# The last 64 tokens of every batch as a ninth batch, and PSUM banks that start from a copy, in an attention and mixer kernel

## The chip, the cores and the metric

The kernel runs on one core of a Trainium2 chip. The metric is the device time of one execution in microseconds. Three runs gave 572.27, 292.12 and 291.67 us; the median is 292.12 us. The profiled execution took 292.22 us, of which the span from the first to the last instruction is 290.5 us. TensorE's granted clock was 1.000 over it.

## What is computed

Eight batches of 576 tokens with eight heads of width 64 go through a block-causal attention (blocks of 64 tokens) and then a mixer: a token MLP over the 576 tokens and a channel MLP over the 512 channels.

```
scores = q @ k.T / 8, masked to block_i >= block_j; attn = softmax(scores); x = attn @ v   # x: 8 x 576 x 512
h  = relu(x.T @ w_tok1) @ w_tok2          # tokens 576 -> 256 -> 576
u  = x + h.T
out = u + relu(u @ w_ch1) @ w_ch2         # channels 512 -> 1536 -> 512
```

Inputs and the output are float32 in HBM; matmul operands are bf16, sums are float32 in PSUM.

## The kernel before

All work is recorded as operations with a list of engines, a cost, what they depend on, a priority, and the PSUM banks that they take and give back. A planner (`Plan.run`) then plays the engines forward on those costs and writes out one fixed order for each engine; the chip runs each engine's list in that order, and semaphores hold an instruction until what it needs is there. `SHIFTS` moves each operation's priority, and `ONLY` ties an operation that may go to VectorE or ScalarE to one of them. So an edit of the operations re-orders everything.

**Attention.** A batch is done in two groups of four heads. q and k come by GpSimd's DMA queue (L491) into `raws`, three buffers each, and VectorE transposes them 32 by 32 into `turned` (L514), three buffers each. TensorE makes scores in 32-row tiles (L638), ScalarE takes exponentials (L656), VectorE copies and clears a corner of the tile (L664, L669, the "tail"), TensorE multiplies by v (L684, and L737 for the last 64 tokens), and VectorE divides (L704, L710, L759, L765).

**Token MLP.** L879 and L883 go up, L976 goes down, L991 adds x. A batch has 4 chunks of 128 tokens, and 64 tokens more. The 64 tokens of two batches make one chunk of 128 (L1007, L1016), called mixed. From the third batch on, u is transposed to `uT` (and `umT` for the mixed chunk) by DMA; before that by TensorE (L1065).

**Channel MLP, up.** Batches 0 to 3 use plain products, 48 matmuls of 512 columns each (L1102, evacuated with a relu by L865 or L867 into `gT`). Batches 4 and 5, and 6 and 7, go as pairs by Strassen's scheme with seven products in place of eight (`channel_up_fast`, L1207): twelve blocks in all, each of seven products of two 512-column matmuls into three banks a, c, e. Three times in a block a running sum is copied out of PSUM into float32 scratch (`keep`, L472 or L474), three times a bank is added to such a copy (`join`, L1235, VectorE alone), two clips apply the relu in SBUF (L1248, L1250), and one evacuation has the relu in it. The mixed chunks go up by 48 matmuls of 128 columns each (L1129).

**Channel MLP, down.** Batch 0 and the mixed chunks use plain products (L1422). Batches 1 to 7 use Strassen's scheme again (`channel_down_fast`, L1331): seven products of twelve 256-column matmuls, four operand sums on VectorE (L1315) into a ring of five `sums` buffers, and seven folds on VectorE (L1354) that add a bank into an output buffer of the ring `o_sb` (four buffers). Batch 7 does this in two halves of 128 tokens. SyncE issues the output DMAs (L1376, L1464, L1472).

**Banks.** PSUM has eight banks. Four are the ring `mm`; four hold score pairs (`sc`) until the last scores are done and are then the pool `late`. The weight sums that the up scheme needs (L1161) lie in the memory of `raws`, so they wait for the last transposes. At the start, filler matmuls on zeros (L444, L451) run while nothing else is ready.

Of the kernel before, what the change touches and what calls it, by code (L numbers as in the profile page):

```python
# [30 lines left out]
class Plan:  # L31
# [5 lines left out]
    FIRST = {"POOL": 2.2, "ACT": 0.7, "SP": 0.7}  # L37
    def __init__(self):
        self.ops = []
        self.free = {}  # L40
# [4 lines left out]
    def add(  # L45
        self, engines, cost, emit, deps=(), prio=0.0, take=(), give=(), xfer=None, mode=0, at=0.0,
        urgent=0, until=1e9, quick=False, stick=False,
    ):

        o = Op()  # L50
        o.engines = (engines,) if isinstance(engines, str) else tuple(engines)
        o.cost = cost if isinstance(cost, dict) else {e: cost for e in o.engines}
        o.emit, o.prio, o.take, o.give, o.xfer = emit, prio, take, give, xfer
        o.mode, o.at, o.urgent, o.until, o.quick, o.stick = mode, at, urgent, until, quick, stick
        o.deps = list({id(d): d for d in deps if d is not None}.values())
        o.users, o.n = [], len(self.ops)
        self.ops.append(o)
        return o

# [20 lines left out]
    def run(self):  # L80
        for o in self.ops:
            o.users = []
            need = {}
            for pools, _ in o.take:
                need[pools] = need.get(pools, 0) + 1
            o.need = list(need.items())
# [15 lines left out]
        while left:  # L102
# [13 lines left out]
            for e in ("PE", "ACT", "DVE", "POOL", "SP"):  # L116
# [33 lines left out]
                o.end = busy[e] = t + o.cost[e]  # L150
# [17 lines left out]
                for note in o.give:  # L168
                    heapq.heappush(gives, (o.end + lag * (not o.quick), note["pool"], note["slot"]))
# [14 lines left out]
    0 0 0 1086 0 0 -1796 0 0 -2204 0 0 -436 0 0 -2236 0 -874 1122 0 -1461 -716 0 -57 -676 0 -823 -356 -634  # L184
    -427 -327 -263 -1862 -1168 -1449 -2035 -910 -961 0 0 0 0 0 -455 -1706 1784 0 0 0 0 0 0 0 0 0 0 0 0 0 0 0 0
    0 0 0 0 0 0 0 0 0 0 0 0 0 0 0 0 0 0 0 0 0 0 0 0 0 0 0 0 0 0 0 0 0 0 0 0 0 0 0 0 0 0 0 0 0 0 0 0 0 0 0 0 0
    0 0 0 0 0 0 0 0 0 0 0 0 0 0 0 0 0 0 0 0 0 0 0 0 0 0 0 0 0 0 0 0 0 0 0 0 0 0 0 0 0 0 0 0 0 0 -1759 -2258
    -829 -1773 -745 -600 -518 -403 -408 -435 -478 -330 -234 -318 115 -707 -721 1449 901 360 -2687 1285 -1364
    -2663 -477 -1268 -1711 287 183 60 -1283 -954 -1917 -689 1260 -1321 -3156 -277 -2070 327 -4275 -2077 496
    -958 721 -1027 -4175 -2062 1142 -727 2194 -29 -1726 -2650 1829 285 -2440 -587 561 -1269 -2630 256 -371  # L190
    -2381 -1108 500 -834 1464 -234 -2459 -3607 -433 -116 -1181 -3036 -4652 757 -3135 -1190 1799 -2575 472 511
    -1937 2261 -2334 -1313 -80 283 -1168 -1950 43 -141 -572 904 -1435 -2531 -1785 -705 1388 1245 8 -529 -1166
    122 839 964 1422 961 460 980 153 587 -70 -1841 -1402 4368 1485 -233 -1066 -157 1316 3304 -4269 -2567 -609
    -37 -2795 -1857 -2628 2386 -953 -1988 756 121 794 -1179 508 -1540 396 993 414 1373 -628 3080 -1481 1693
    1380 2018 3179 1215 133 -1865 -30 -1438 310 -1741 1233 2110 3174 952 1308 1314 2083 -536 -1377 2942 3324
    3966 4046 -972 2806 2021 -985 1780 2009 2286 1063 -343 -501 3018 -221 -12 851 -3518 181 648 3044 777 -1559
    1331 2605 -1938 2510 -1273 1427 692 3242 642 3161 831 3827 1590 2498 1272 3666 1243 -521 1458 965 2312
    3170 1911 1539 456 1382 -395 1781 1291 412 1115 2033 407 -2584 203 1653 -37 -1067 651 390 632 712 2085
    1236 1774 1916 638 -351 1999 3579 1238 3795 2213 1760 2315 580 1733 1472 2148 32 1832 1928 3235 2037 1010
    1326 3512 2592 569 1322 795 233 4616 692 2264 1859 3321 2543 1003 -1446 -622 1012 5769 3912 3513 -1135  # L200
    3484 1816 1558 3086 1631 377 460 3746 131 2416 1317 3495 268 93 1492 -2200 1682 -1517 -1061 -1918 -804
    -2555 220 1892 -1350 -552 633 -602 -3011 2584 -1528 1015 -1345 -970 -279 205 -3142 -1238 490 -3231 1304
    -4554 -73 -1779 -1041 -2783 -2072 1282 -1760 -3094 -3999 -1158 -3686 -2285 -1138 2616 668 1259 1241 -1598
    167 2071 -909 858 -881 727 2164 -1678 1042 574 -585 -480 1799 -693 -2709 29 2701 348 589 1804 2316 358
    -243 1501 498 -1435 2925 2117 -1872 -1946 -1387 -550 71 3572 -327 523 -486 285 2909 1867 3747 1873 -3277
    -237 -2256 -2904 165 1714 -375 2033 1315 108 1985 908 -3282 871 -1113 -3213 -1928 456 -985 -2942 -1169
    -1109 -439 -1452 -1077 1083 4521 -657 -397 -1807 -1177 148 -136 72 -499 -383 2346 -1426 535 908 1654 -1908
    1556 -870 940 1384 760 3049 1518 1614 -388 -397 698 599 -1772 77 -1100 -188 -99 1679 -537 3661 -611 -4713
    -2779 -3471 -1192 4222 -2288 7 135 683 470 -124 -1937 4311 -1202 2026 3954 1883 -580 -144 -1263 -1252 213
    124 -1229 1816 -503 66 -1382 -2249 -465 -2153 -1738 2390 -2661 -24 -2228 -2001 -239 -409 -1529 -375 -1081  # L210
    -581 735 -984 38 -260 -2302 1217 -2261 -3269 -2251 -248 -4644 -204 -1377 -2426 -4000 -3533 -8 -1126 -1048
    1395 -1267 -1990 -1332 -2616 -192 -1101 44 -647 1960 -632 -3925 1998 -2860 -1766 -1304 1946 -86 -1897 1720
    -2063 220 166 1393 1695 678 281 1263 937 1502 1991 1492 1224 967 -2008 -3069 100 -1197 831 -2311 762 2963
    -2753 1116 -1491 772 -1270 -2454 -83 -684 517 2274 -199 924 -996 -335 -437 -4244 92 2836 34 1600 1818
    -1703 782 437 3822 -1486 158 903 133 149 -809 -2686 1861 1030 754 81 904 4463 -1403 3008 -481 2513 2124
    362 2078 2881 2322 87 45 1400 1014 -40 -952 494 -2798 1008 -114 697 3665 -1141 -790 980 3595 2615 768 1541
    2162 1088 350 4168 2791 198 819 1089 1662 127 -873 -1414 -1490 -607 1650 -475 -1425 155 -479 819 -205 3125
    1025 1982 -966 1282 523 1433 -866 2401 -1302 -2306 -1390 1706 -1061 492 -1463 362 -5 -382 4027 670 261
    -1148 3368 3865 226 2561 -27 918 1300 -1251 479 -1039 -942 377 1706 -1619 634 2612 294 -1198 -454 -443
    3079 257 2561 367 4603 1450 1230 175 3506 2620 1475 2517 1440 -455 1815 2349 469 1362 -2181 3618 1351 245  # L220
    2103 3448 -649 1023 -389 1673 1698 1565 3393 -672 -617 1513 1982 1900 -43 -2127 -515 177 1287 -662 3642
    435 -281 523 1100 -3212 -53 930 2250 -1503 -2709 -312 1997 -1218 -146 -1266 500 -430 -294 -3993 259 38
    3742 2116 492 3949 930 120 -982 1354 3674 845 2860 394 407 2113 2870 17 2438 -399 5223 4732 5550 4129 4822
    -33 2182 140 2669 2676 1714 -1974 3137 2139 597 3962 -795 -837 -175 1231 2212 -2167 872 1722 1254 1464
    2663 -1228 3092 1502 3237 3444 837 1937 1623 4494 3997 1526 2423 2361 3182 5805 -2367 3270 4613 6090 1790
    -279 1558 -1156 3445 2684 5301 1696 3189 2135 3585 4003 1969 -123 4948 2149 90 3310 -2135 1890 2816 3455
    3645 1607 1958 2568 1525 -862 -700 1980 4204 3729 2032 1434 102 -1352 1072 -305 329 2181 3132 -214 1770
    3447 1290 174 -1834 3312 -2908 2149 2971 -366 1171 1119 2325 -854 967 2462 -356 1390 9 1911 1872 1049 -29
    1500 -1830 879 -556 946 -2641 1129 89 -1773 630 -830 307 -726 612 -2751 -266 -369 -2652 -249 -2997 -2094
    -899 -3813 -1242 -82 -2802 -4725 -1627 -158 -2687 -3327 -1181 -2531 223 -1599 2803 -1175 -2176 -1434 -2276  # L230
    -4223 -5240 341 496 422 482 -3394 -3204 -2712 -2522 -2522 -1911 -658 -1781 -2177 653 0 -882 1808 55 1483
    -527 1255 -875 -780 -1430 -1339 427 -56 -728 -1932 -2188 1432 -2375 1447 -1541 -275 -412 1347 1940 -1648
    1054 -2047 -2930 -20 -638 -3394 -289 236 1329 -396 -1030 -2 -444 2933 1287 2625 1732 2239 -2641 1568 -100
    2268 1855 -176 2627 -458 1457 325 641 3791 -1272 2191 1450 850 1534 2275 1760 1242 3001 2749 4305 1003
    2517 -1573 -478 2960 949 -609 376 1575 1763 -2541 -909 -788 -97 -352 -310 862 -3721 -1923 635 -135 1667
    574 1186 2265 115 611 666 -636 1650 2081 -469 1899 -579 -251 -160 -1812 4751 1754 904 2662 2274 -443 4012
    415 477 1333 2156 1991 2662 2996 269 1798 748 3408 -2292 -1115 735 2456 2953 43 -2067 -63 -553 1093 719
    -283 929 -1465 841 -2035 -1822 -1363 -820 -2068 -704 -3580 -995 -5820 -1642 692 -1374 -1445 -1196 -624
# [29 lines left out]
def kernel(  # L268
# [11 lines left out]
    nc = tc.nc  # L280
# [1290 lines left out]
```

## Time and profile before

| | |
|---|---|
| Median of the runs shown | 292.12 us |
| Profiled execution, its span | 292.22 us, 290.5 us |
| TensorE busy | 283.6 us (98%), 3991 matmuls |
| VectorE busy | 242.3 us (83%) |
| ScalarE busy | 150.5 us (52%) |
| GpSimd busy | 62.4 us (21%) |
| Down products by Strassen (L1331) in the chain that ended last | 17.8% + 4.1% of the span |
| Plain up products (L1102) in it | 14.9% |
| Up products by Strassen (L1207) in it | 6.4% + 6.1% |
| Mixed chunk, up (L1129), in it | 3.5% |

Busy time is the time in which at least one of an engine's instructions ran. Matmuls overlap each other in the records, since each is listed from its start to the modelled end of its output, so the time that one costs is read from how far apart the starts of equal matmuls lie, not from its listed length. The chain that ended last is followed back from the last instruction to what released each step.

### The profile page before, as it was taken

Reading aid. Unit: us, or ns where it says so; the run is one execution under the profiler, and the core shown is the slowest. Engines: PE = TensorE matmul, PEld = TensorE weight load, DVE = VectorE, ACT = ScalarE, POOL = GpSimd, SP = SyncE. Lnnn points to the kernel's source line nnn. Section 1 sums busy time; section 2 is a strip of 40 time slices with the busy share of each in tenths; the row PEclk is TensorE's granted clock in tenths of the full one; section 3 lists DMA queues with packets and bytes.
Section 4 is the critical chain, followed back from the end, with each engine's and each line's share of the span. In section 5 each row is a group of like instructions: output and inputs, shape, how many; then the busy total and the mean of one; then the engine's idle time right before and its main releaser. Section 6 shows DMA issues by size and latency. Waiting matters only on the chain.

```text
span 290.5 us, 9147 instructions
## 1 busy us (share of the span) xinstructions
PE 283.6 (98%) x3991; PEld 186.4 (64%) x3991; DVE 242.3 (83%) x520; ACT 150.5 (52%) x196; POOL 62.4 (21%) x101
## 2 busy tenths in 40 slices
PE   8999999899999999999999999999999999999994
PEld 3576555556746676565877576875456897555884
DVE  3686498786899998789999866998999969999993
ACT  5985727487636556765576976503536102545000
POOL 9674455550170035142005000000000000000000
PEclk9999999999999999999999999999999999999999
DMA  7999999999299059989927800610101921310134
GB/s 234 210 167 202 211 194 192 224 189 161 45 103 178 0 89 192 190 121 172 81 76 99 60 2 2 93 74 9 64 20 24 150 45 74 144 72 2 37 112 180
DMA packets 64840, 32.67 MB, mean 112 GB/s; under 512 B 53152, under 2 KB 55328, under 8 KB 64800
## 3 DMA queue, kind: packets, MB, share of 16 engines
q0 software_dynamic: 44032, 16.75, 49.3%
q1 hardware_dynamic: 20768, 15.34, 21.7%
q8 instruction: 31, 0.51, 0.7%
q14 instruction: 9, 0.07, 0.1%
HBM read 35.85 MB, written 9.44 MB: 156 GB/s over the span
## 4 chain that ended last, share of the span: by engine, by line
PE 95%; DMA 2%; ACT 1%; DVE 1%; issue 1%; SPq 0%
PE mm L1331 18%; PE mm L1102 15%; PE sc L638 11%; PE mm L1422 7%; PE mm L684 7%; PE mm L1207 6%; PE late L1207 6%; PE mm L879 5%; PE late L1331 4%; PE mm L976 4%; PE mm L1129 3%; PE mm L737 3%; DMA gT<-in_q_dram 2%; PE mm L883 1%; PE mm L451 1%; PE mm L1007 1%
## 5 line engine op out<-in xcount | busy, mean ns | idle before, releaser
L656 ACT ACTIVATE e_sb<-sc 128x1024 bf16<-128x1024 f32 x95 | 92.2, 1023 | 44.4 <-PE sc L638 41.3
L1102 PE MATMUL mm<-uT,wc_sb 128*128 128x512 bf16 x192 | 46.6, 381 | 0.0
L540 POOL DMA_DIRECT2D vals<-in_v_dram x45 | 37.0, 834 | 39.3 <-PE mm L684 27.9
L514 DVE STREAM_TRANSPOSE turned<-raws 128x288 int32<-128x288 int32 (+1 forms) x65 | 40.6, 695 | 5.6 <-ACT raws L472 4.2
L638 PE MATMUL sc<-turned 32*64 32x64 bf16 (+7 forms) x1260 | 35.0, 292 | 0.5 <-DVE turned L514 0.5
L1102 PEld LDWEIGHTS <-wc_sb 128*128 128x128 bf16 x192 | 20.0, 115 | 16.5 <-issue 1.9
L638 PEld LDWEIGHTS <-turned 32*64 32x64 bf16 x1280 | 19.5, 104 | 14.5 <-issue 10.9
L684 PE MATMUL mm<-vals,e_sb 128*128 128x65 bf16 x630 | 25.9, 193 | 1.3 <-issue 1.3
L710 DVE TENSOR_TENSOR x_sb<-mm,rinv 128x256 bf16<-128x256 f32 x63 | 25.8, 420 | 1.3
L684 PEld LDWEIGHTS <-e_sb 128*128 128x128 bf16 x640 | 23.1, 97 | 5.6 <-issue 2.3
L1331 PEld LDWEIGHTS <-sums 128*128 128x128 bf16 x252 | 24.3, 98 | 3.4
L1331 PEld LDWEIGHTS <-gT 128*128 128x128 bf16 x240 | 22.8, 98 | 4.6 <-issue 0.4
L867 DVE TENSOR_SCALAR gT<-mm 128x512 bf16<-128x512 f32 x25 | 17.2, 689 | 9.5 <-PE mm L1102 9.1
L865 ACT ACTIVATE gT<-mm 128x512 bf16<-128x512 f32 x26 | 15.6, 600 | 6.0 <-PE mm L1102 4.8
L879 PE MATMUL mm<-x_sb,w_sb 128*128 128x512 bf16 (+1 forms) x88 | 17.1, 321 | 0.0
L1354 DVE TENSOR_TENSOR o_sb<-mm,u_sb 128x512 f32<-128x512 f32 x22 | 15.1, 686 | 2.1 <-PE mm L1331 1.9
L1331 PE MATMUL mm<-wd_sb,sums 128*128 128x256 bf16 x132 | 16.4, 273 | 0.0
L991 DVE TENSOR_TENSOR u_sb<-mm,x_sb 128x512 bf16<-128x512 f32 x23 | 15.2, 684 | 0.9 <-PE mm L976 0.7
L1207 PEld LDWEIGHTS <-raws 128*128 128x128 bf16 x96 | 9.2, 98 | 10.1 <-issue 0.2
L865 ACT ACTIVATE aT<-mm 128x512 bf16<-128x512 f32 (+1 forms) x12 | 6.3, 526 | 18.1 <-PE mm L883 18.1
L1331 PE MATMUL mm<-wd_sb,gT 128*128 128x256 bf16 x120 | 14.7, 273 | 0.0
L472 ACT COPY e_sb<-mm 128x512 f32<-128x512 f32 x8 | 4.7, 588 | 19.4 <-PE mm L1207 19.3
(156 smaller groups left out, 490.1 us busy)
## 6 DMA issues: line engine op xcount, KB each, us to landing
out_dram<-o_sb SPq DMA_DIRECT2D x14, 512.0 KB, 3.0
raws<-in_k_dram POOLq DMA_DIRECT2D x14, 288.0 KB, 7.8
raws<-in_q_dram POOLq DMA_DIRECT2D x14, 288.0 KB, 7.1
vals<-in_v_dram POOLq DMA_DIRECT2D x28, 128.0 KB, 7.1
wc_sb<-in_moe_w_ch_dram POOLq DMA_DIRECT2D x8, 192.0 KB, 8.3
wc_sb<-in_moe_w_ch_dram POOLq DMA_DIRECT2D x3, 512.0 KB, 11.4
out_dram<-o_sb SPq DMA_DIRECT2D x10, 128.0 KB, 2.3
gT<-in_k_dram SPq DMA_DIRECT2D x4, 288.0 KB, 3.9
```

Of the source, the lines that this page charges most:

```text
L514: nc.vector.transpose(dst[:, 0:S, :] .rearrange("p s e -> p (s e)") .bitcast(I32) .rearrange("p (a k) -> p k a", k=NB)[:, k0:k1], raw2.bit ...
L540: nc.gpsimd.dma_start(out=t[128 - p : 128, J, hs, 0:64], in_=src)
L638: nc.tensor.matmul(out=home(n)[64 * half : 64 * half + 64, c : c + w], lhsT=bar[r, 0] if j is None else kT[i][r, 64 * j : 64 * j + 64, par ...
L656: nc.scalar.activation(dst, sc[SC.index(note["pool"])][:, :, 0:n], EXP, scale=scale)
L684: nc.tensor.matmul(out=u[:, I, 0:65], lhsT=e[:, h, c : c + 128], rhs=vt[:, J, head, 0:65], start=(J == 0), stop=(J == I),)
L710: nc.vector.tensor_tensor(out=xt[:, 0:4, 64 * head : 64 * head + 64], in0=u[:, :, 0:64], in1=ri[:, 0:4].to_broadcast([128, 4, 64]), op=MULT,)
L865: nc.scalar.activation(dst, src, RELU)
L879: nc.tensor.matmul(out=ps, lhsT=w1_sb[:, c, tt : tt + 255 : 2], rhs=xt[:, c, cols], start=(c == 0), stop=False)
L1102: nc.tensor.matmul(out=bank_of(bank), lhsT=wc1_sb[:, m, channels(cc)], rhs=uT[b % 2][:, :, m, :], start=(m == 0), stop=(m == NDM - 1),)
L1207: nc.tensor.matmul(out=bank_of(bank), lhsT=x(m), rhs=y[:, :, m, :], start=first and m == 0, stop=m == 1, skip_group_check=not first,)
L1331: nc.tensor.matmul(out=bank_of(bank)[:, 256 * i : 256 * i + 256], lhsT=x[:, kk, 128 * i : 128 * i + 128], rhs=y[:, kk], start=first and i ...
L1422: nc.tensor.matmul(out=ps, lhsT=gt[:, cc, c0 : c0 + 128], rhs=wc2_sb[:, cc, cols], start=(cc == 0 and not turned), stop=(cc == NDC - 1),)
```

## The change

- The 64 last tokens of all eight batches are collected in `um_sb` and `umT`, four chunks of 128, and treated as a ninth batch of 512 tokens. It goes up by a new function, `channel_up_half`, with Strassen's scheme over the two token halves (seven products of four 256-column matmuls in each of three blocks), and down by `channel_down_fast`. `channel_up_mixed` and the mixed branch of `channel_down` are gone; what is left of the latter is `first_down` for batch 0.
- In both up schemes and in the down scheme, a running sum that two results share is no longer copied to SBUF and added back by VectorE. It is copied from its bank into a second bank (`seed`), and the following matmuls add onto that bank. One `keep` stays in an up block in place of three, two joins in place of three, one clip in place of two, and two evacuations with the relu in place of one. In a down block a copy replaces one of the seven folds. An up block now has four banks (a, e, c, d).
- The planner keeps banks that a 512-column matmul covered last (`full`, `late`) apart from the others (`mm`, `late mm`). It gives seeded banks from the first kind where it can, and the kernel issues a 512-column identity matmul (`cover`) where it can't, before the copy goes in.
- Rings: q and k have two raw and two turned buffers in place of three, `sums` three in place of five, `o_sb` three in place of four. The scratch for `keep` is six single tiles. The weight sums for the up scheme get their own memory and are made from the second batch on.
- The tail's copy and clear may run on GpSimd. Costs in the planner are a little different, and `SHIFTS` and `ONLY` are new throughout.

```diff
+    def bare(self, note):
+        return note.get("seed", False) and note["pool"] in ("mm", "late mm")
...
-    raws = sb.tile([128, 6, NB * D], BF16, name="raws")
-    turned = sb.tile([128, 3, 2 * S, 2], BF16, name="turned")
+    qk_sb = sb.tile([128, 2 * QK, 2, NB * D], BF16, name="qk_sb")     # QK = 2
-    ws_sb = raws.rearrange("p n c -> p (n c)")[:, 0 : 4 * DC].rearrange("p (n m c) -> p n m c", n=4, m=2)
+    ws_sb = sb.tile([128, 4, 2, DC // 2], BF16, name="ws_sb")
+    th_sb = sb.tile([128, 3, 2, 2, 128], BF16, name="th_sb")
+    half = ring(2, [128, 2, 256], FP32, "half")
-    um_sb = ring(2, [128, DM], BF16, "um_sb")
+    um_sb = sb.tile([128, 4, DM], BF16, name="um_sb")
-    umT = ring(1, [128, NDM, 128], BF16, "umT")
+    umT = sb.tile([128, 4, NDM, 128], BF16, name="umT")
-    sums = ring(5, [128, NDC // 2, 256], BF16, "sums")
-    o_sb = ring(4, [128, 2, DM], FP32, "o_sb")
+    sums = ring(3, [128, NDC // 2, 256], BF16, "sums")
+    o_sb = ring(3, [128, 2, DM], FP32, "o_sb")
...
+    SEED = ("full", "late", "mm", "late mm")
+    def cover(bank):
+        if P.bare(bank):
+            nc.tensor.matmul(out=bank_of(bank), lhsT=ident, rhs=wc1_sb[:, 0, 0:512], start=True, stop=True)
...
-        copied = P.add("DVE", 0.16, emit_copy, deps + list(et_war), prio, urgent=urgent)
+        copied = P.add(TAILS, {"DVE": 0.15, "POOL": 0.4}, emit_copy, deps + list(et_war), prio, urgent=urgent)
...
     def channel_up_fast(b, uT_done, wc1_ready, prio):
...
-            r1 = keep(0, "a", product(0, "a", a_of(0, 0), b11, base))
-            r6 = keep(1, "e", product(1, "e", s_of(0), t[0], [made[0]] + ws_ready))
-            r2 = keep(2, "a", product(3, "a", s_of(1), t[1], [made[1]] + ws_ready))
-            r5 = join(0, c1, 0, "c", [product(2, "c", a_of(0, 1), b21, base), r1], True)
-            clip(0, slice(c1, c1 + 1), [r5])
-            r7 = join(1, c1, 2, "e", [product(4, "e", s_of(3), b22, base + ws_ready), r2], True)
-            r3 = join(1, c2, 1, "a", [product(5, "a", s_of(2), t[2], [made[2]] + ws_ready), r6], False)
+            op = product(0, "a", a_of(0, 0), b11, base)
+            r1 = keep(product(1, "e", s_of(0), t[0], [made[0], op] + ws_ready))
+            seed("c", op)
+            seed("d", product(3, "a", s_of(1), t[1], [made[1]] + ws_ready))
+            final(0, c1, "c", product(2, "c", a_of(0, 1), b21, base))
+            r7 = join(1, c1, "d", [product(4, "d", s_of(3), b22, base + ws_ready), r1], True)
+            r3 = join(1, c2, "a", [product(5, "a", s_of(2), t[2], [made[2]] + ws_ready), r1], False)
             clip(1, slice(c1, c2 + 1, 2), [r7, r3])
-            op = product(6, "a", a_of(1, 1), t[3], [made[3]] + wc1)
+            final(0, c2, "a", product(6, "a", a_of(1, 1), t[3], [made[3]] + wc1))
...
     def channel_down_fast(b, g_done, wc2_ready, u_done, prio):
...
-            fold("a", 0, 0, product(0, "a", a11, b11), True, False)
+            op = product(0, "a", a11, b11)
+            def emit(o, nt=nt, banks=banks):
+                src, dst = (bank_of(banks[to])[:, 0 : 256 * nt] for to in "ac")
+                cast(o, dst, src)
+            last["a"] = last["c"] = P.add(EVAC, evac_cost(256 * nt), emit, [op], prio - 1)
+            fold("c", 0, 0, product(0.5, "c", a12, b21), True, True)
...
-            fold("c", 0, 0, product(5, "c", a12, b21), False, True)
+            for row in range(2) if b == B else ():
+                for kk in range(2):
+                    def emit(o, row=row, kk=kk):
+                        nc.sync.dma_start(
+                            out=out[4 * row + kk : 4 * row + 4 : 2, 512:576, :].rearrange("t i d -> i t d"),
+                            in_=o_sb[oi[row]][64 * kk : 64 * kk + 64],
+                        )
...
-            if p % 2 == 1:
-                gm_done = channel_up_mixed(p // 2, um_done, wc1_ready, 10 * p + 3.5)
-                channel_down(p, gm_done, wc2_ready, um_rows, prio, mixed=True)
             if p == B - 1:
+                gm_done = channel_up_half(B, um_all, wc1_ready, MIXED[0])
+                channel_down_fast(B, gm_done, wc2_ready, um_rows_all, MIXED[1])
                 channel_down_fast(p, g_done, wc2_ready, u_done, 10 * p + 4)
```

The new up function, cut to its products (`t` are four token-side sums made by VectorE, L1166 of the changed kernel):

```
def channel_up_half(b, uT_done, wc1_ready, prio):
    ...
    for k in range(NDC // 4):                                  # three blocks
        banks = {to: {"covers": True, "seed": to in "cd"} for to in "aecd"}
        def product(i, to, x, y, deps):
            ...
                for o_ in range(2):
                    for m in range(2):
                        nc.tensor.matmul(out=bank_of(bank)[:, 256 * o_ : 256 * o_ + 256], lhsT=x(o_, m), rhs=y[:, :, m, :], ...)
        op = product(0, "a", a_of(0, 0), b11, base)
        r1 = keep(product(1, "e", s_of(0), t[0], [made[0], op] + ws_ready))
        seed("c", op)
        seed("d", product(3, "a", s_of(1), t[1], [made[1]] + ws_ready))
        final(0, 0, "c", product(2, "c", a_of(0, 1), b21, base))
        r7 = join(0, 1, "d", [product(4, "d", s_of(3), b22, base + ws_ready), r1], True)
        r3 = join(1, 1, "a", [product(5, "a", s_of(2), t[2], [made[2]] + ws_ready), r1], False)
        clip(0, 2, 1, [r7, r3])
        final(1, 0, "a", product(6, "a", a_of(1, 1), t[3], [made[3]] + wc1))
```

## The prediction

> **What bounds the kernel.** I read the busy times first.
>
> ```profile
> PE 283.6 (98%) x3991; PEld 186.4 (64%) x3991; DVE 242.3 (83%) x520; ACT 150.5 (52%) x196; POOL 62.4 (21%) x101
> ```
>
> TensorE is busy 98% of the span, but matmuls overlap in the records, so this could hide idling. Two views decide it. The waits of TensorE, all of them (what it waited for, total, times, longest):
>
> ```profile
> PE mm L684 <- issue: 1.3, 1, 1.3
> PE mm L444 <- DVE wd_sb L418: 1.2, 1, 1.2
> PE sc L638 <- DVE turned L514: 0.5, 1, 0.5
> ```
>
> Two lie in the first 9 us; only one, 1.3 us, lies behind them. And busy time by stretches of 20 us (length; PE, weight loads, DVE, ACT, POOL; clock, DMA):
>
> ```profile
> 60.00:80.00 20.00, 20.00 (x393) 13.52 (x392) 15.49 (x42) 15.34 (x20) 4.10 (x6) 1.00 0.89 128
> ...
> 240.00:260.00 20.00, 20.00 (x125) 12.40 (x124) 19.12 (x33) 8.46 (x13) 0.00 (x0) 1.00 0.28 105
> 260.00:280.00 20.00, 20.00 (x159) 14.92 (x158) 19.50 (x36) 5.23 (x8) 0.00 (x0) 1.00 0.13 40
> ```
>
> From 60 us on TensorE has work in every microsecond. VectorE is nearly full late on (19.1 and 19.5 of 20) and still never holds TensorE. The chain of waits gives the real price of matmuls, since there they stand one behind another (start, length, what):
>
> ```profile
> 64.69 0.89 PE mm L1129 x16
> ...
> 91.94 0.86 PE mm L1422 x4
> ...
> 93.38 2.73 PE mm L1331 x24
> ...
> 139.96 2.62 PE mm L1331 x24
> ...
> 188.91 1.31 PE mm L1331 x12
> ```
>
> So a 512-column matmul costs 0.215 us, one of 256 columns 0.109 us, one of 128 columns 0.056 us. The 24 at 93.38 come right behind a score set and cost 0.11 us more than the 24 at 139.96: that is the price of going from small tiles back to the full array. With these prices the matmuls from the first L1102 (26.9 us) to the end of the list (286.6 us) fill the stretch to within about half a microsecond. **The kernel is bound by TensorE's issue, without slack**; only fewer matmul columns can shorten it, and any new wait on TensorE shows in full.
>
> **The change, part by part.** Counts are of the built programs.
>
> *Matmuls.* Removed: 192 of 128 columns (L1129), 12 groups of 16 at 0.89 = 10.68 us; 48 of 512 columns (the mixed half of L1422), 12 groups of 4 at 0.86 = 10.32 us. Together 21.00. Added: 84 of 256 columns in the new up function and 84 in the down scheme, 14 groups of 12 at 1.31 = 18.34 us. Net **-2.66 us**. The pair blocks keep their 168 matmuls, the down scheme its seven products. No identity matmul for a seeded bank stands in the changed program. Passages from small tiles to the full array go from 56 to 55: -0.11 us. Four more filler matmuls stand at the start, where nothing else is ready: nothing.
>
> *Seeds.* 39 copies from bank to bank, 28 on ScalarE and 11 on VectorE. No such copy is in the trace. The nearest rows are copies from PSUM to SBUF of the same size:
>
> ```profile
> L472 ACT COPY e_sb<-late 128x512 f32<-128x512 f32 x13 | 7.4, 589 | 12.4 <-PE late L1207 12.4
> ...
> L474 DVE COPY e_sb<-late 128x512 f32<-128x512 f32 x6 | 4.0, 688 | 0.3 <-PE late L1207 0.2
> ```
>
> I take 0.59 and 0.69 us. The bounds are the spacing of back-to-back operations (0.49 and 0.60), and twice the rows (1.2 and 1.4), if reading and writing PSUM should exclude each other. The new wait: product 2 must wait for the copy of product 0, and all of TensorE's list stands behind it. A result is seen by VectorE 0.20 us after the last issue (286.76 against 286.55 at the end), so a copy needs 0.20 + 0.69 + about 0.06 = 0.95 us. In the changed order at least 1.30 us of other matmuls (three products of 0.43) lie between a pair block's product and the next user of its copy, as before. Cost: nothing, unless the copies take over 1 us.
>
> *Other engines.* VectorE: 161 operations of 512 elements from PSUM in place of 172, -7.6 us at 0.687; tails to GpSimd, 9 x 0.226 + 8 x 0.165 = -3.4; sums of the ninth batch 4 x 0.95 + 4 x about 0.4 (estimate, below the 0.55 of the 768-wide ones) = +5.4; the 256-wide and clips about zero. VectorE falls from 242 to about 237 us, and the 3.8 us of up-weight sums move from 161-170 us to the early part. ScalarE: 23 evacuations more at 0.59 less about 5.5 of clips, 150 to 159 us. Neither is the bound, so this is worth nothing, but the cover gets thicker exactly where VectorE was full. What TensorE would wait for next isn't there: TensorE is already the end of the line.
>
> *Tails on GpSimd.* No row shows them; nearest are 0.31 us (memset 64x256) and 0.29 (select 128x128), against 0.23 and 0.17 on VectorE. Bounds: -0.2 us and +0.6 for a pair. Behind them in GpSimd's list stand the q, k and v loads, and score exponentials before them. TensorE's list has other matmuls there: nothing.
>
> *Two q and k buffers.* Loads land late:
>
> ```profile
> out_dram<-o_sb SPq DMA_DIRECT2D x14, 512.0 KB, 3.0
> raws<-in_k_dram POOLq DMA_DIRECT2D x14, 288.0 KB, 7.8
> ...
> out_dram<-o_sb SPq DMA_DIRECT2D x3, 256.0 KB, 2.3
> ```
>
> In the changed order the shortest room behind the opening, from a load's issue to the transpose that needs it, is 10.4 us of matmuls, against 7.8 us median and 12.0 us at most over all loads into `raws`. Before, most had 12 us or more. Nothing by the median; up to 2 us at two or three places by the maximum.
>
> *Three output buffers.* The last batch's fold into a buffer that the ninth batch still sends has 3.1 us of matmuls behind the issue of that DMA. Landing takes 2.3 us (256 KB) to 3.0 us (512 KB), and an issue some 0.5 us before it. Before, the shortest such room was 4.4 us. Folds give banks back, so VectorE's list and then TensorE's would stand: 0 to 0.7 us, I take **+0.3**. The three `sums` buffers leave 5.9 us at the tightest, for one 0.95 us sum: nothing.
>
> Sum: -2.66 - 0.11 + 0.3 = -2.5 us on the profiled 292.22 us, that is **289.7 us**. The profiled execution is 0.1 us from the median of the runs, so the same number stands for that.
>
> **Rivals.**
>
> *Seeds need a matmul each.* The code issues a 512-column identity matmul for a seeded bank that the planner does not know as covered. If each of the 39 seeded banks needed one, TensorE would get 39 x 0.215 = 8.4 us: 298.1 us. The built order has none, and the planner tracks which banks a whole matmul covered last; nothing in the trace of before can show more. Chance 0.01. [...]
>
> *Copies between banks are slow (ends slower than before).* A pair or ninth-batch block hangs on bank a: four products of 0.43, two copies, a join and an evacuation, about 5.2 us by the rows, and two blocks are in flight, so 2.6 us for each 3.0 us of matmuls. If a copy takes d longer than 0.6, each of the 15 blocks takes d longer per pair of copies and two blocks, so TensorE stands d - 0.4 us per block. It eats the 2.5 us at d = 0.57, a copy of 1.2 us, and decides from there; copies of 1.4 us give 15 x 0.4 = 6 us, 295.7. For it: no such copy was seen. Against it: ScalarE's and VectorE's rows hardly differ between forms of equal size. Chance 0.08.
>
> *Shorter rings hold TensorE.* Two or three late q or k loads of 1 to 2 us, or 0.7 us and more at the output buffers: +2 to +4, 291.5 to 293.5 us. For: the rooms above are the shortest in the changed order. Against: TensorE's list has had only one wait in 280 us. Chance 0.18.
>
> *More goes.* The single 1.3 us wait at 53.6 us, in the midst of equal matmuls and released by nothing, may fall elsewhere; the opening, where 17.5 us of matmul work takes until 26.9, may come out 1 us shorter, with all four `uT` copies on ScalarE: 286 to 288 us. Chance 0.14.
>
> **The numbers.** Forecast 289.7 (288 to 291.3), chance 0.59; the rivals as given. The range 286.8 to 293.3 holds the forecast, most of the short rings and the gain, and leaves out about 0.17. A measurement of this kernel can tell about 2%, 5.8 us: under 286.3 is faster, over 298.0 slower. Faster 0.06 (the end of the gain case), slower 0.05 (slow copies at their worst, covers), same 0.89.
>
> **What would show it.** TensorE's waits still near 3 us in all; the 256-column matmuls at 0.109; seeds near 0.59 and 0.69 us; 20.00 of 20 busy from 60 us to the last 10; VectorE near 237 us. I am wrong if TensorE waits for folds, seeds or transposes after 30 us, if VectorE waits for an output DMA near the end, or if the first plain up product comes later than 27 us.

## The result, and the profile after

The changed kernel takes 288.38 us (median of four runs, 287.65 to 289.13), the kernel before 292.27 us on the same chip: a ratio of 0.9874, with a 95% interval of 0.983 to 0.9917. One of the four runs of the kernel before took 572.27 us and is not in the ratio. That is 3.9 us less, where the forecast was 2.5 us less than 292.22 us. A gain of 1.3% is under the 2% from which the prediction speaks of faster, so it counts as the same, as forecast; the interval still lies wholly under 1. The profiled execution took 287.65 us with a span of 285.7 us, 4.8 us under the span before.

The first lines are again the busy times and all waits of TensorE in the changed kernel (what it waited for, total us, times, longest).

```profile
PE 280.5 (98%) x3923; PEld 188.2 (66%) x3923; DVE 234.5 (82%) x498; ACT 157.9 (55%) x212; POOL 69.6 (24%) x118
```

```profile
PE mm L469 <- DVE wd_sb L443: 1.2, 1, 1.2
PE sc L664 <- DVE qk_sb L540: 0.2, 1, 0.2
```

The wait of 1.3 us amid the products of attention and values (L684, now L712) is gone, and no wait for a seed, a fold or an output buffer has come. VectorE has 7.8 us less to do, ScalarE and GpSimd a little more. Busy time by stretches (length; PE, weight loads, DVE, ACT, POOL; clock, DMA share, GB/s) shows TensorE as full as before:

```profile
60.00:80.00 20.00, 20.00 (x385) 12.26 (x383) 14.57 (x39) 16.85 (x22) 4.03 (x9) 1.00 0.78 127
100.00:120.00 20.00, 19.93 (x371) 12.45 (x366) 15.74 (x41) 14.35 (x18) 11.57 (x17) 1.00 1.49 199
240.00:260.00 20.00, 20.00 (x124) 12.41 (x123) 18.66 (x32) 10.90 (x19) 0.00 (x0) 1.00 0.00 1
260.00:280.00 20.00, 20.00 (x186) 17.93 (x184) 17.96 (x34) 0.36 (x1) 0.00 (x0) 1.00 0.33 106
```

And the chain of waits has the same prices of matmuls (start, length, what): twelve of 256 columns 1.31 us, the twelve right behind small tiles 0.11 us more, four plain ones of 512 columns 0.86 us.

```profile
60.01 0.86 PE mm L1547 x4
...
88.61 2.62 PE mm L1452 x24
91.81 1.42 PE mm L1452 x12
93.52 1.31 PE mm L1452 x12
...
171.71 2.73 PE mm L1452 x24
```

Since TensorE's list is one unbroken row, the time from the start of each matmul to the start of the next can be summed by line in both traces. That tells where 4.83 us of the two profiled lists went:

| matmuls | before, us | after, us | difference |
|---|---|---|---|
| plain down (L1422, L1547) | 21.04 | 10.75 | -10.30 |
| mixed chunk up, ninth batch up (L1129, L1194) | 10.77 | 9.17 | -1.60 |
| Strassen down (L1331, L1452) | 64.51 | 73.92 | +9.40 |
| attention times values (L684, L712) | 23.01 | 21.44 | -1.57 |
| its blocks of two (L737, L765) | 7.41 | 6.91 | -0.50 |
| plain up, scores, Strassen up of the pairs | | | -0.23, -0.19, -0.10 |
| all others | | | +0.25 |

The first three rows are what the change says it does: -2.50 us. The fourth holds the vanished wait: the 1.32 us of idle time, and 0.16 us that its last matmul takes longer to be followed, 1.48 us from start to start. What the change does with the seeds, the price list of copies, is in the groups of instructions (operation, count, busy us, mean ns, idle time before them):

```profile
L498 ACT COPY mm<-late 128x512 f32<-128x512 f32 x14 | 8.0, 577 | 10.4 <-PE late L1318 8.5 <-DVE mm L500 1.1 <-PE late L1452 0.7
L500 DVE COPY mm<-mm 128x512 f32<-128x512 f32 x5 | 3.5, 693 | 0.8 <-PE mm L1318 0.8
L500 DVE COPY mm<-late 128x512 f32<-128x512 f32 x5 | 3.4, 696 | 0.2 <-PE late L1318 0.2
...
L690 POOL COPY vals<-e_sb 128x256 bf16<-128x256 bf16 x9 | 4.8, 533 | 30.6 <-ACT e_sb L682 30.5
L695 POOL MEMSET e_sb<- 64x256 bf16 x8 | 2.5, 312 | 3.4 <-DVE vals L690 3.1
```

A copy from bank to bank takes 577 ns on ScalarE and 693 to 696 on VectorE, within 2% of the 589 and 688 ns of the same copies into SBUF. So the fewer columns explain 2.5 us. Of the profiled lists 2.3 us are left, 1.48 of them the stall; of the medians 1.4 us were open.

### The profile page after: what moved, and what is told of

It is laid out like the page before. It is cut to its first block, busy times and chain, and to the rows that moved or that the text cites. A ratio compares the mean times of both kernels' runs of the same rounds, so it can differ in the third digit from the quotient of the medians.

```text
span 285.7 us, 9042 instructions
## 1 busy us (share of the span) xinstructions
PE 280.5 (98%) x3923; PEld 188.2 (66%) x3923; DVE 234.5 (82%) x498; ACT 157.9 (55%) x212; POOL 69.6 (24%) x118
## 4 chain that ended last, share of the span: by engine, by line
PE 96%; DMA 1%; DVE 1%; SPq 0%; ACT 0%; issue 0%
PE mm L1452 17%; PE mm L1125 15%; PE sc L664 11%; PE late L1452 9%; PE mm L712 8%; PE late L1318 7%; PE mm L1318 6%; PE mm L906 5%; PE mm L1001 4%; PE mm L1547 4%; PE mm L765 2%; PE mm L1194 2%; DMA gT<-in_q_dram 1%; PE mm L910 1%; PE late L1194 1%; PE mm L476 1%
## 5 line engine op out<-in xcount | busy, mean ns | idle before, releaser
L540 DVE STREAM_TRANSPOSE qk_sb<-qk_sb 128x288 int32<-128x288 int32 (+1 forms) x65 | 41.2, 695 | 7.2 <-ACT qk_sb L498 4.0
L664 PE MATMUL sc<-qk_sb 32*64 32x64 bf16 (+7 forms) x1260 | 34.8, 293 | 0.2 <-DVE qk_sb L540 0.2
L1125 PEld LDWEIGHTS <-wc_sb 128*128 128x128 bf16 x192 | 20.2, 115 | 17.2 <-issue 1.3
L1452 PEld LDWEIGHTS <-sums 128*128 128x128 bf16 x288 | 27.7, 98 | 4.1 <-issue 0.9
L1452 PEld LDWEIGHTS <-gT 128*128 128x128 bf16 x288 | 27.5, 98 | 3.8
L664 PEld LDWEIGHTS <-qk_sb 32*64 32x64 bf16 x1280 | 19.6, 104 | 14.2 <-issue 9.0
L894 DVE TENSOR_SCALAR gT<-mm 128x512 bf16<-128x512 f32 x25 | 17.2, 687 | 13.9 <-PE mm L1125 13.2
L712 PE MATMUL mm<-vals,e_sb 128*128 128x65 bf16 x640 | 27.0, 193 | 0.1
L712 PEld LDWEIGHTS <-e_sb 128*128 128x128 bf16 x640 | 23.8, 97 | 4.8 <-issue 1.2
L892 ACT ACTIVATE gT<-mm 128x512 bf16<-128x512 f32 x35 | 20.5, 604 | 8.6 <-PE mm L1125 4.0
L498 ACT COPY mm<-late 128x512 f32<-128x512 f32 (+1 forms) x15 | 8.4, 563 | 26.3 <-PE late L1452 16.5
L1452 PE MATMUL mm<-wd_sb,sums 128*128 128x256 bf16 x132 | 16.4, 273 | 0.0
L1318 PEld LDWEIGHTS <-ws_sb 128*128 128x128 bf16 x96 | 9.4, 98 | 9.9
L517 POOL DMA_DIRECT2D qk_sb<-in_k_dram x14 | 7.7, 553 | 32.8 <-DVE qk_sb L540 24.0
L1001 PE MATMUL mm<-aT,w_sb 128*128 128x512 bf16 x56 | 14.1, 380 | 0.0
L1452 PE MATMUL mm<-wc_sb,gT 128*128 128x256 bf16 x108 | 13.3, 273 | 0.0
```

What stands on the lines that cost most here:

```text
L540: nc.vector.transpose(dst[:, 0:S, :] .rearrange("p s e -> p (s e)") .bitcast(I32) .rearrange("p (a k) -> p k a", k=NB)[:, k0:k1], raw2.bit ...
L664: nc.tensor.matmul(out=home(n)[64 * half : 64 * half + 64, c : c + w], lhsT=bar[r, 0] if j is None else kT[i][r, 64 * j : 64 * j + 64, par ...
L712: nc.tensor.matmul(out=u[:, I, 0:65], lhsT=e[:, h, c : c + 128], rhs=vt[:, J, head, 0:65], start=(J == 0), stop=(J == I),)
L892: nc.scalar.activation(dst, src, RELU)
L1001: nc.tensor.matmul(out=bank_of(bank), lhsT=w2_sb[:, t, 128 * si : 128 * si + 128], rhs=at[:, t, :], start=(t == 0), stop=(t == NDT - 1),)
L1125: nc.tensor.matmul(out=bank_of(bank), lhsT=wc1_sb[:, m, channels(cc)], rhs=uT[b % 2][:, :, m, :], start=(m == 0), stop=(m == NDM - 1),)
```

## The experiments

Three theories stand against each other. **Columns**: TensorE has no slack, so the gain is matmuls. **Relief**: the gain, or a part of it, comes from VectorE or the new order. **A stall that comes and goes**: the 1.3 us of the profile before are no property of the old order, but were lost by chance. Four kernels ran first on one chip, beside 15 runs of the kernel before (median 292.6 us).

### The price of a matmul ahead of each seed

```diff
     def cover(bank):
-        if P.bare(bank):
+        if True:
             nc.tensor.matmul(out=bank_of(bank), lhsT=ident, rhs=wc1_sb[:, 0, 0:512], start=True, stop=True)
```

> The changed kernel, with the 512-column matmul issued ahead of every one of the 39 seeded banks instead of none: 39 x 0.215 = 8.4 us of matmul more, nothing else altered. Theory (TensorE is bound by issue and has no slack, so columns are time, one to one): about 288.4 + 8.4 = 296.8 us, between 296.2 and 297.4, and the seeds wait for nothing new. Rival (TensorE only looks busy and the limit is VectorE or the order, so that some of the matmuls fall into time that is lost anyway): less than 293.

Measured: 297.03 us, ratio to before 1.0181 (1.0133 to 1.0229), 8.2 us over the 288.82 us of the changed kernel on this chip. TensorE's waits:

```profile
PE mm L469 <- DVE wd_sb L443: 1.2, 1, 1.2
PE mm L712 <- issue: 0.4, 1, 0.4
```

39 matmuls at 0.215 us are 8.4 us, and that is what they cost, one to one. It bears out "columns", and it sizes the rival that seeds need a matmul each: the changed kernel would have been slower than before by 1.8%. The changed kernel's 39 seeds are running sums, and none has such a matmul ahead of it: the planner gives them banks that a matmul of 512 columns covered last.

### The same seeds, each copied twice

```diff
-                    cast(o, bank_of(dst), bank_of(src))
+                    for _ in range(2):
+                        cast(o, bank_of(dst), bank_of(src))
```

> The changed kernel, with each of the 39 seed copies made twice in a row, so that a seed takes 1.17 us on ScalarE and 1.39 us on VectorE instead of 0.58 and 0.69; the matmuls are the same. Theory (the copies lie beside 1.3 us of other matmuls and cost nothing until one takes about 1.2 us): 0 to +3 us, most likely +1.5, so 288.4 to 291.4, all of it as waits of TensorE for the seeds of VectorE. Rival A (the copies are on the path now, and what the change gained was cut by them): +39 x 0.6 = +23 us, about 311. Rival B (nothing but matmuls counts, whatever the copies take): 288.4 within 0.3 us.

Measured: 295.68 us, ratio 1.0102 (1.0077 to 1.0127), 6.9 us over the changed kernel. The waits of TensorE, in the pair blocks' products (L1319):

```profile
PE mm L1319 <- DVE mm L500: 1.4, 4, 0.5
...
PE late L1319 <- DVE late L500: 0.9, 1, 0.9
...
PE mm L1319 <- ACT mm L498: 0.6, 1, 0.6
PE late L1319 <- DVE mm L500: 0.3, 1, 0.3
```

By the starts of the matmuls, TensorE stood 6.0 us in 16 pieces of 0.09 to 1.07 us before products of the up schemes. None of the three expectations holds: the copies are neither free at twice their length nor on the path as a whole. The forecast had said that a copy costs nothing "unless the copies take over 1 us", and its rival let a copy of 1.2 us eat 2.5 us in all, 0.17 us for each of the 15 blocks; the expectation of this run put the start of harm at about 1.2 us. The first agrees with both doublings, the other two were too mild. Most waits name VectorE, though it makes only 11 of the 39, so a new question came up: does the length of each block's chain do it, or VectorE's full list?

> The changed kernel with only the 28 seed copies that stand on ScalarE made twice (15.7 us of ScalarE more); the 11 on VectorE are made once. With all 39 doubled, TensorE stood 6.0 us more in 16 pieces between the products of the pair blocks. Theory 1 (the pieces come from the chain of each block, product, copy, next product, which every doubled copy lengthens alike): a share of 15.7 / 23.3 of them stays, +4.0 us, about 292.5. Theory 2 (they come from VectorE, which has no free time there, so that each VectorE copy pushes back every evacuation behind it, while ScalarE has room): +0 to +1.5 us, 288.4 to 290, and nearly no wait for a ScalarE seed.

This kernel doubles only the copies on ScalarE (`for _ in range(2 if o.engine == "ACT" else 1)`). Measured: 292.21 us, ratio 0.9982 (0.9961 to 1.0003), about 3.5 us over the changed kernel.

```profile
PE mm L1319 <- ACT mm L498: 1.1, 2, 0.6
...
PE mm L1194 <- ACT mm L498: 0.2, 1, 0.2
```

TensorE stood 3.3 us in 12 pieces in the same products, now waiting for ScalarE. ScalarE has more idle time than this (busy 60% of the span), so it is the chain that counts, theory 1. The forecast's own sum gives the size, worked out after the runs: 0.20 us until the result is seen, the copy, 0.06 us (the two waits for VectorE in the profile before ended 0.05 to 0.06 us after its end), against 1.30 us of other matmuls. Twice 0.58 us oversteps by 0.12 us, times 28 is 3.4 us; twice 0.69 us by 0.34 us, times 11 is 3.7 us; together 7.1. The sums fit 3.3 and 6.0 roughly, but the pieces are uneven, so the sum isn't the mechanism in detail.

### Only the columns of the change, in the kernel before

```diff
+                        top = NDC - 3 if mixed else NDC
-                        for cc in range(4 * part, 4 * part + 4):
+                        for cc in range(4 * part, min(4 * part + 4, top)):
```

> The kernel before, with the last three of the twelve 512-column matmuls left out in each of the four products of last tokens on the way down (12 of 48 matmuls, so these rows of the output lack a quarter of their sum); order, copies and rings are those of before. It takes 12 x 0.215 = 2.6 us of matmul away, as the change does by 2.66, and nothing of what else the change does. Theory (the gain is the columns): 292.3 - 2.6 = 289.7 us, 289.4 to 290.0. Rival (the gain comes from relief of VectorE, the seeds or the new order): 291.5 to 292.3.

Measured: 290.5 us, ratio 0.9927 (0.9899 to 0.9955), 2.1 us less than before. The interval, 1.3 to 3.0 us, holds the 2.6 us and shuts out "relief", which had at most 0.8 us, but the value is above the range that I gave. The profiled execution (290.84 us) offers a reason: it holds two stalls of the kind in question, 1.4 us at L684 as before and 0.5 us more at L737. Whether the other executions hold both isn't known.

```profile
PE mm L684 <- issue: 1.4, 1, 1.4
PE mm L444 <- DVE wd_sb L418: 1.2, 1, 1.2
PE mm L737 <- issue: 0.5, 1, 0.5
```

### The tails back on VectorE

```diff
+            if op.engine == "POOL" and op.emit.__qualname__.split(".<locals>.")[-2] == "tail":
+                op.engine = "DVE"
             op.emit(op)
```

> The changed kernel with the 9 copies and 8 clears of the exponentials' last columns issued on VectorE at the same places of its list instead of on GpSimd, which gives VectorE 3.4 us more. Theory (TensorE is the bound, and VectorE has room in the stage of the scores): 288.4 within 0.7 us, no new wait of TensorE. Rival (the gain came from relief of VectorE): up to +3.4 us, 291.8.

Measured: 289.11 us, ratio 0.9867 (0.9824 to 0.991), against 0.9861 for the changed kernel on the other chip (0.2 us), with no new wait but the stall (here 1.6 us). VectorE's relief in the score stage is worth nothing that can be seen.

### The stall that comes and goes

> The changed kernel once more, with more executions. Theory (a stall of TensorE of 1.3 us, which the profile of before has at 53.4 us between two matmuls of one group, where nothing holds it but its own instructions, comes in some executions of this kernel and not in others): the times fall into two groups 1.2 to 1.4 us apart, about 287.7 and 289.05, and the profiled one shows the stall if it is of the upper group and not if it is of the lower. Rival (the spread is even): times between 287.5 and 289.2 without a gap, and a stall in the profile that does not go with the time.

The changed kernel once more: 287.47, 287.96, 288.72, 288.91, 289.47 and 289.48 us, median 288.82, ratio 0.9861 (0.9836 to 0.9886). There are no two groups with a gap, so that part fell. But the profiled execution (288.72 us) has a stall, in another place than the profile before. The timeline of TensorE, first before, then in this run (start, length, what; in brackets the idle time ahead and what ended it):

```profile
53.16 0.45 PE L684 MATMUL mm<-vals,e_sb 128*128 128x65 bf16 x9
54.93 0.20 PE L684 MATMUL mm<-vals,e_sb 128*128 128x65 bf16 x1 [1.32 <-issue]
```

```profile
20.67 0.39 PE L712 MATMUL mm<-vals,e_sb 128*128 128x65 bf16 x7
22.07 0.55 PE L712 MATMUL mm<-vals,e_sb 128*128 128x65 bf16 x13 [1.01 <-issue]
```

Each time a head's row of ten matmuls is cut, where the code asks for no wait. Before, 862 matmul records lie ahead of the cut, here 350. The difference is 512, four times 128, and both numbers are 94 above a multiple of 128. The page of before lists a DMA queue of instructions (packets, MB, share):

```profile
q8 instruction: 31, 0.51, 0.7%
```

That is 31 fetches of 16,384 bytes; the 3991 matmuls and 3991 weight loads of before make 257 TensorE instructions to each of them. So if all of them bring TensorE's instructions, a fetch brings about 128 matmuls with their loads, an estimate from this count, and the cuts lie at one phase of it. The times of the traces:

```
kernel          cut behind record   fetch runs      next matmul   from the fetch's end
before                  862         52.65-53.54        54.93          1.39
cover_all               350         20.08-21.02        22.32          1.30
seeds_twice             350         20.57-21.52        22.88          1.36
before_cut              350         19.76-20.72        22.15          1.43
after_again             350         19.71-20.69        22.07          1.38
scalar_twice            350         19.66-20.61        22.07          1.46
tails_vector            350         20.92-21.90        23.17          1.27
after_third             350         19.99-20.95        22.30          1.35
after            (350, no cut)      19.01-19.96        21.27          1.31
```

TensorE resumes 1.27 to 1.46 us after the end of one fetch, whatever the length of the stall (0.2 to 1.6 us). In the first profile of the changed kernel the fetch came just early enough: the 350th matmul started at 21.10, the next at 21.27 us. (The second cut of before_cut, with five records missing, fits with 1.27 us.) The places without a cut bear it out. Seven profiles hold every matmul, with 206 such places in all; the matmul behind the place never starts sooner than 1.27 us after the end of its fetch, but for one that starts after 1.11 us, in the split kernel below, where the cut comes one matmul later.

This also shows where a good part of the even spread comes from. Four profiles of the changed kernel (one with a little traffic added at 155 us) take 287.65, 288.49, 288.72 and 288.58 us; their matmul behind the 350th starts at 21.27, 21.56, 22.07 and 22.30 us, and from there to the last matmul they need 260.4 to 261.0 us. Their first scores start at 7.85, 8.26, 7.61 and 8.67 us: a late opening leaves a short stall, or none, and an early one runs into the wait for the fetch.

If this is right, the stall belongs to a place in the stream of instructions and not to a place in the program. So the stream was shifted, by more instructions of the same columns at its start:

```diff
-                nc.tensor.matmul(out=bank_of(bank), lhsT=zeros[:, 0:128], rhs=zeros, start=True, stop=True)
+                for k in (0, 256):
+                    nc.tensor.matmul(
+                        out=bank_of(bank)[:, k : k + 256], lhsT=zeros[:, 0:128], rhs=zeros[:, k : k + 256],
+                        start=True, stop=True,
+                    )
```

and the 256-wide fillers likewise into two of 128.

> The kernel before, with each of the 43 first matmuls (which only keep TensorE busy until data lands) split into two of half the width: the same columns, 43 pairs of instructions more ahead of everything. So far every stall of TensorE within a group of equal matmuls that was over 0.5 us came behind matmul record 350 or 862 of the list, both 94 more than a multiple of 128, in kernels whose lists differ there; 128 matmuls with their 128 weight loads are one instruction fetch of 16 KB. Theory (TensorE has run out of fetched instructions at the edge of a chunk): if a stall comes, it comes again behind a record number that is 94 above a multiple of 128 (a few less where records are missing), so 43 matmuls earlier in the program's own order, and not at the group at 53.4 us; the time is 290.7 to 293 according to whether the fetch now meets less traffic. Rival (something at that place of the program holds TensorE): the stall stays between the same two matmuls, then about record 905, 9 above a multiple of 128, and the time is 292.5.

> The changed kernel with the same split of its 47 first matmuls. Theory (chunks of instructions): a stall, if there is one, comes behind a record number that is 94 above a multiple of 128, and not behind the matmul that was number 350; the time stays within 287.4 to 289.5, as the parts of the work are the same. Rival (a place in the program): the stall stays at the matmul that was number 350, now about 397, 13 above a multiple of 128.

Measured: before_split 290.88 us (eight runs, 290.37 to 291.41), ratio 0.9926 (0.9904 to 0.9949); after_split 287.82 us (287.57 to 288.19), ratio 0.9821 (0.9775 to 0.9867). The waits of the split kernel before, in full, and of the split changed kernel:

```profile
PE mm L445 <- DVE wd_sb L418: 1.2, 1, 1.2
```

```profile
PE mm L470 <- DVE wd_sb L443: 1.2, 1, 1.2
PE sc L669 <- DVE qk_sb L545: 0.2, 1, 0.2
PE mm L717 <- issue: 0.2, 1, 0.2
```

Neither has a cut over 0.2 us, and the stall did not stay with its matmul, as the rival had it. The 0.2 us of after_split is a cut of the same kind at another matmul of the program: it comes behind record 351, 95 above a multiple of 128, and 1.49 us after the end of a fetch. The second fetch starts at 17.2 and 17.6 us here, against 19.0 to 20.9 us in the table.

With nothing but fillers altered, the kernel before loses 1.85 us (292.73 to 290.88 us). Not all of it is traced. The profiled lists of before and before_split differ by 0.90 us: the products with v take 1.74 us less (1.48 of it the stall), the fillers with the wait for the first scores 0.64 us more, the scores 0.19 us more, and every other row is the same within 0.01 us. So in these executions the split took the stall away and paid about half of the gain back at the opening and in the scores; what a stall costs in a typical run isn't shown. Between the two split kernels, whose profiles hold no stall over 0.2 us, the change is worth 290.88 - 287.82 = 3.06 us.

> The changed kernel with its 47 first matmuls split into two, once more, beside the changed kernel itself on the same chip. Theory (the split moves the edges of the chunks off the crowded moment): 287.5 to 288.3 in every execution, without a stall. Rival (the four even times of before were luck): some executions above 288.6.

> The changed kernel itself, for comparison with its split form on the same chip. Theory: 287.4 to 289.5, executions with and without the stall; median 0.5 to 1.2 us above the split form. Rival: the same as the split form.

Measured on another chip: after_split_again 288.3 us (287.7 to 288.82), ratio 0.9838 (0.9813 to 0.9864); after_third 288.86 us (288.58 to 289.28), ratio 0.9859 (0.9837 to 0.9882). The split form is again ahead, by 0.6 us, but two of its four times are over 288.6 us, as the rival had it. The profiled one (287.97 us) has no stall; whether the two others have one, or only a late opening, isn't known. The split form is the fastest version here, and its lead over the changed kernel, 0.6 us on this chip and 1.0 us when taken from two chips, is within the intervals.

### Why the fetch is late

In the profiles so far all stalls lie in the first 56 us, where the DMA engines are full (share 1.22, 1.18 and 1.63 of the changed kernel in 0 to 20, 20 to 40 and 40 to 56 us). The stretch from 100 to 120 us of the changed kernel has a share of 1.49 too, and no stall for which the profile names no engine. So the fetch might wait among the packets of the loads, or its moment might be set by TensorE's own list; full DMA engines alone make no stall there. Two kernels were to tell the two apart, and neither did.

> The changed kernel with the channel weights not loaded: each of the 11 loads (192 KB x 8 and 512 KB x 3, which land between 15 and 45 us) is replaced by a fill with a constant on GpSimd at the same place, so the output is computed with other weights; the work of TensorE, VectorE and ScalarE is the same. [...]

Measured: 298.67 us (five runs, 295.2 to 301.81); the ratio, from the three shortest, is 1.0132 (1.008 to 1.0184). The fills did something else. GpSimd's and VectorE's instructions (start, length, what) and TensorE's longest wait:

```profile
16.97 4.22 POOL L600 MEMSET wc_sb<- 128x768 bf16 x6
21.04 1.90 POOL L606 MEMSET wc_sb<- 128x2048 bf16 x1
...
23.31 1.90 POOL L606 MEMSET wc_sb<- 128x2048 bf16 x1
```

```profile
16.69 8.58 DVE L684 COPY vals<-e_sb 128x128 bf16<-128x128 bf16 x1
16.86 8.41 DVE L781 RECIPROCAL rinv<-mm 128x1 f32<-128x1 f32 x1
25.36 0.11 DVE L689 MEMSET e_sb<- 64x64 uint32 x1
```

```profile
PE mm L706 <- DVE x_sb L787: 7.3, 1, 7.3
```

A VectorE copy that takes 0.22 us in the changed kernel (L690 there, 128x128) stood 8.6 us beside the fills, TensorE waited 7.3 us behind it, and its granted clock reads 0.74 in the stretch from 20 to 40 us. The second fetch ran at 19.62 us, among the 19.0 to 20.9 us of the table; but loads still filled the DMA engines in that moment (share 0.8 to 1.2 from 15 to 20 us), so the run does not decide. Nor is the profile free of stalls: one of 0.3 us comes at 58.3 us among the scores, behind record 729 (with four missing, 93 above a multiple of 128), 1.34 us after the end of a fetch.

> The changed kernel with two loads more on GpSimd's queue, of 2304 packets of one element each, into a small tile that nothing reads. They are issued behind the eighth of the nine clears of tails, at about 155 us, from where until about 171 us the DMA engines stand still otherwise. Nothing else is altered. [...]

Measured: 288.49 us in its one run. No trace shows when a fetch is asked for, so its start is counted here from the matmul that has 55 more than a multiple of 128 ahead of it, a place of the author's choice. The packets of the traffic ran until 160.7 us and so met one fetch alone, which started at 160.6 us, 2.1 us behind that matmul, against 1.0 to 1.3 us in three profiles without the traffic. The next, without traffic, started 1.2 us behind. So the one is later, but the traffic was over when it began, and this run does not decide either, though the fetch began just when the packets ended. The place lies too early, which the record shows: in the first profile of the changed kernel the fetches at 197.3 and 253.6 us start 6.0 and 6.3 us behind it while the DMA engines stand still. Counted from the 86th matmul behind a multiple of 128 instead, the 11 fetches of that profile that come with the DMA engines idle (share of at most 0.02) start between 1.2 us ahead and 0.5 us behind; the 19 others start 0.7 to 4.6 us behind, those of the first 56 us 1.8 to 4.5 us. So in this profile fetches come later where the DMA engines are busy. Whether the loads make them late stays open, as traffic and stage change together; shown is when TensorE resumes behind a late one, 1.27 to 1.49 us after its end.

## Why the prediction was right, and where it was off

The time lies in the range, and its likeliest case came: TensorE as bound, fewer columns, no new wait. By its steps:

- *What bounds the kernel.* Right. 39 matmuls added cost 8.2 of 8.4 us, and 12 left out give 2.1 of 2.6; 3.4 us of VectorE's work put back cost some 0.2 us, less than the runs can tell.
- *Matmuls, -2.66 us.* The sums of starts give -2.50 us. The 0.11 us for one passage fewer can't be told apart.
- *Seeds, nothing.* Right. The copies took 0.58 and 0.69 us as taken from the rows of copies to SBUF, and TensorE waited for none. The doubled ones bracket the limit: with 0.69 us no cost, with 1.16 us for the 28 on ScalarE 3.3 us. The rival of slow copies names the right mechanism, but its price per block was too low.
- *Other engines.* VectorE was forecast at 237 us and is at 234.5, ScalarE at 159 and is at 157.9. Neither holds TensorE.
- *Tails on GpSimd, nothing.* The copy took 533 ns and the clear 312, against 241 ns for the same copy on VectorE, all of it hidden.
- *Two q and k buffers, nothing.* The only wait of TensorE for a transpose is 0.2 us (0.5 before). Loads landed in 6.3 and 6.9 us (median).
- *Three output buffers, +0.3 us.* **This term failed.** TensorE waited for no fold in the profile after, so it was nothing, though the transfers took longer than forecast (3.4 us for 512 KB, 3.3 us for 256 KB, against 3.0 and 2.3). One later profile, of the split form, has 0.2 us for a fold.
- *The single 1.3 us wait.* **The missing term.** The sum left it in both kernels, and the rival "more goes" had it go with a chance of 0.14. By the author's reading of the table it is a late fetch of instructions: TensorE resumed 1.27 to 1.49 us after the end of one. It did not go: it moved to another matmul, and most later profiles of the changed kernel and its variants have it, with 0.2 to 1.6 us. The first profile was a lucky one. Splitting the fillers is worth 1.85 us in the kernel before, and 0.6 us in the changed one, each on one chip; nothing in the change's design aims at this difference, so it is luck.

So of the 3.9 us about 2.5 are columns, which is shown. About 0.8 (3.9 less 3.06) goes away when the fillers of both kernels are split, and is most likely a smaller stall; that is argued, from medians of different chips. About 0.5 remains between the split kernels (3.06 less 2.50): in their profiles it lies in pieces of 0.1 to 0.5 us in the rows of attention and plain up, and its cause is open. The number was within the range because the main term was right.

## What to carry to other kernels

Where one engine issues without a gap, price a change by that engine's list alone, and test the price by adding the work rather than by trusting the busy share. A copy from one PSUM bank into another cost here what a copy to SBUF costs (0.58 and 0.69 us against 0.59 and 0.69), and it was free where its length plus about 0.3 us fitted under the matmuls between its source and its user. A wait "for issue" in the midst of equal matmuls is worth counting: if the number of matmuls ahead of it keeps its remainder by 128 from kernel to kernel (94 here), look for a fetch of instructions that ended just ahead of it (1.27 to 1.49 us here); a few more instructions at the start may move it away.

## What the runs showed of the hardware

The cuts in TensorE's list without a named cause came 94 matmuls above a multiple of 128 (93 and 95 once each), and ended 1.27 to 1.49 us after a 16 KB fetch. That TensorE had run out of instructions there is the author's reading; no profile names the cause. That a shift of 43 instruction pairs is worth 1.85 us was not expected.

A bf16 copy on VectorE, 0.22 us in the changed kernel, took 8.6 us beside fills on GpSimd: it ended at 25.27 us, and a whole row of eight fills, from 16.97 to 25.21 us, with the issue of a load among them, ran in that time.

In the stretch of that stop, from 20 to 40 us, the granted clock reads 0.74, and 0.983 as the mean of the span; in the other profiles the mean is 0.998 or more.
